# Two weight blocks kept in PSUM: other blocks, other slots, and three small moves in the loop's dependency chain

## The chip, the cores and the metric

One core of a Trainium2 chip. The metric is the device time of one execution in microseconds; lower is better. In this kernel TensorE does the matrix products, VectorE, ScalarE and GpSimd the copies and the softmax, and SyncE issues the transfers (DMA) from HBM, the memory off the core; SBUF is the on-chip memory that holds the weights, PSUM the smaller one that the products write to. Where I quote a ratio, it is the mean time of one kernel's fast runs over that of the other kernel's fast runs of the same rounds, so it is not quite the ratio of the medians beside it. Sessions ran on different chips (the kernel before had medians from 2851.5 to 2869.2 us in them), so kernels are compared by their ratios to the kernel before, or within one session.

Times inside a step are counted from the write of `hT`, the first thing that the next step's products need. Where I say "mean of the steps", I took the trace's records of 58 or 59 steps and laid them over each other at that write; first and last packets of a block were found by counting the 4096-byte packets, 128 to a block, in the order of their starts, and are medians over the steps. Issue times are means.

## The reference, cut to what matters

Two independent parts are joined along the last axis. Part B is a long convolution that the change does not touch. Part A is attention with a memory that is handed from one segment of 32 rows to the next, so its 64 steps run one after the other:

```python
mem = mem0
for s in range(n_seg):                                  # 64 steps
    h = concatenate([mem, x[s]], axis=1)                # 8 + 32 rows
    q, k, v = (einsum('btd,dhe->bhte', h, W) for W in (Wq, Wk, Wv))
    p = softmax(where(mask, q k^T * scale, -1e9))
    o = einsum('bhqk,bhke->bhqe', p, v)
    o = einsum('bhte,hed->btd', o, Wo)
    mem = o[:, :8, :]                                   # the next step waits for this
    outs.append(o[:, 8:, :])
```

Each step needs all four weights, 64 blocks of [128, 2048] bf16 (512 KB). They do not all fit on chip.

## The kernel before: what the change touches

46 of the 64 blocks stay in SBUF for the whole loop. 16 are streamed from HBM in every step, in a fixed order, through four buffers ("slots") in turn. The last two are *kept*: they lie in PSUM, and VectorE copies each of them in every step to one of the four slots, after that slot's streamed block was used and before its next load.

```python
STREAM = {("k", 0): (0, 6), ("q", 0): (3,), ("k", 1): (0, 4), ("q", 1): (0, 4), ("v", 0): (0, 4), ("v", 1): (0, 4)}
STREAM_O = (0, 4, 8, 11, 14)
KEPT = {("k", 0, 4): ("o", 14), ("q", 0, 5): ("k", 0, 6)}    # kept block: whose slot it is copied to
SLOTS = 4

def unit(key):                                 # the weights of one block, just before their products
    if key in W_res: return W_res[key]
    if key in kept:  return ahead_of.pop(key)
    between.pop(key, lambda: None)()           # other DMAs that go into the queue ahead of this load
    place[key] = loads[0] % SLOTS; loads[0] += 1
    t_ = wst.tile([128, 2048], BF16, name="wst", tag="w%d" % place[key])
    nc.sync.dma_start(out=t_[:], in_=WD[key][:])
    return t_

def fetch(key):                                # copy a kept block, as int32 words, into a slot
    t_ = wst.tile([128, 2048], BF16, name="wst", tag="w%d" % place.get(KEPT[key], SLOTS - 1))
    for n in range(2):
        words(t_[:, 1024 * n:1024 * n + 1024], kept[key][n][:])
    ahead_of[key] = t_
```

All loads go through one queue, SyncE's, in program order. A load waits there until its slot is free, and every later load waits behind it. With 16 loads and four slots, slot 0 takes in each step k0's first block, k1's fifth, v0's fifth and o's fifth; slot 1, among others, k0's seventh and q1's first; slot 2 q0's fourth and q1's fifth; slot 3 k1's first, v0's first and the last streamed o block (the names of the loads in a step are, in order: k0_0, k0_6, q0_3, k1_0, k1_4, q1_0, q1_4, v0_0, v0_4, v1_0, v1_4, o0, o4, o8, o11, o14). I use these names below, and the same kind of name for kept blocks.

The step itself (cut; `...` marks cuts):

```python
between["k", 1, 0] = lambda: stores(s - 1, ob)          # the last step's two stores, ahead of k1_0
a = quads("k", 0, range(KC))
...
fetch(("q", 0, 5))
k0 = evac(a, "A")
...
a = quads("k", 1, H0); ...; quads("k", 1, H1, a)        # H0 = 0..3, H1 = 4..7
...
tr(p1, 0, k1, KT1[:, :, :, 0:SL])                       # VectorE copies the transposes
S0 = softmax_b(st0, ex0)
...
L0 = left_blocks(S0)
quads("v", 0, H1, a); V0 = evac(a, "A")
sc1 = scores(1, QT1, KT1); st1, ex1 = softmax_a(sc1)
...
nc.vector.tensor_copy(out=hT[:, :, XM:SL]..., in_=pt_o[...])   # the hT write
fetch(("k", 0, 4))
```

## Time and profile before

| | before |
|---|---|
| device time, median of 3 | 2859.5 us |
| loop, period of a step (mean of 62) | 27.37 us |
| weights streamed in a step | 16 x 512 KB |
| DMA engines idle in a step (mean of the 16) | 2.66 us |
| of that, excess in the 2nd to 4th us after the hT write | 0.74 us |
| TensorE waits for streamed blocks | 3.7 us a step |

The lines behind it are in the prediction. The rows of idle time are no lines of a view: they are 16 less the number of packets of SyncE's queue under way, summed over time, divided by 16, as a mean of the steps.

### The profile page before, as it was taken

What the parts mean: (1) busy time and instruction counts of PE and PEld (TensorE: products, weight loads), DVE (VectorE), ACT (ScalarE), POOL (GpSimd) and SP (SyncE); (2) the same over time, 40 slices, a digit from 0 to 9 for tenths busy, and PEclk for the clock granted to TensorE, in tenths of its full rate; (3) what the DMA queues carried; (4) which work ended last, traced back from release to release, by engine and by line L of the source; (5) the groups of instructions that cost most, each with busy time, mean ns of one, the idle gap of its engine ahead of it and who ended that gap; (6) DMA issues with size and microseconds to landing.
All of it is one profiled execution on the core that took longest, in us unless ns stands there. A gap on an engine that the chain in (4) does not pass through costs nothing. (4 is left out here: it accounts for less than half of the span.)

```text
span 2863.4 us, 75870 instructions
## 1 busy us (share of the span) xinstructions
PE 2100.6 (73%) x32791; PEld 1102.1 (38%) x32838; DVE 1511.0 (53%) x2882; ACT 976.7 (34%) x1458; POOL 365.3 (13%) x545
## 2 busy tenths in 40 slices
PE   1478777756797478778777877887787777778747
PEld 0246444542243134344443443443444434344323
DVE  7577677765985145445444444444444444454430
ACT  4767688751121122222222222222222222222220
POOL 2254444542000100000000000000000000000000
PEclk8699888977899799999999999999999999999978
DMA  4556554525345899989989999998999998999991
GB/s 111 149 153 171 168 165 128 148 78 162 99 133 187 318 321 329 320 305 332 320 316 332 329 320 320 327 339 298 330 319 311 331 317 315 320 328 336 322 315 42
DMA packets 377504, 734.83 MB, mean 257 GB/s; under 512 B 115958, under 2 KB 208118, under 8 KB 375120
## 3 DMA queue, kind: packets, MB, share of 16 engines
q1 hardware_dynamic: 352866, 679.52, 70.4%
q0 software_dynamic: 8528, 28.41, 2.8%
q10 hardware_dynamic: 15774, 22.03, 2.4%
q8 instruction: 257, 4.21, 0.6%
q14 instruction: 79, 0.65, 0.1%
HBM read 675.04 MB, written 67.37 MB: 259 GB/s over the span
## 5 line engine op out<-in xcount | busy, mean ns | idle before, releaser
L310 PE MATMUL acc<-wst,hT 128*32 128x512 bf16 x3328 | 371.0, 402 | 235.1 <-DMA wst<-WD_k 132.8
L310 PEld LDWEIGHTS <-hT 128*32 128x32 bf16 x12288 | 318.7, 98 | 560.7 <-issue 288.5
L316 ACT CAST ev<-acc 128x512 bf16<-128x512 f32 x384 | 225.1, 586 | 511.5 <-PE acc L310 509.0
L409 PEld LDWEIGHTS <-oT 128*32 128x32 bf16 x8192 | 204.2, 96 | 169.8 <-issue 119.8
L310 PE MATMUL acc<-W_q,hT 128*32 128x512 bf16 x3072 | 242.6, 390 | 0.0
L310 PE MATMUL acc<-W_k,hT 128*32 128x512 bf16 x2816 | 237.4, 404 | 0.0
L409 PE MATMUL pp<-W_o,oT 128*32 128x256 bf16 x5632 | 223.0, 273 | 0.0
L261 DVE TENSOR_SCALAR wst<-keep 128x512 int32<-128x512 int32 x256 | 165.0, 686 | 106.8 <-PE acc L310 82.9
L310 PE MATMUL acc<-W_v,hT 128*32 128x512 bf16 x3072 | 213.6, 382 | 0.0
L348 DVE TENSOR_REDUCE mx<-sc 128x8 f32<-128x320 f32 x128 | 62.3, 487 | 242.2 <-PE sc L341 242.1
L409 PE MATMUL pp<-wst,oT 128*32 128x256 bf16 x2560 | 128.0, 276 | 77.7 <-DMA wst<-WD_o 64.7
L322 DVE COPY KT<-tr 128x512 bf16<-128x512 bf16 x128 | 54.4, 425 | 211.7 <-PE tr L321 211.7
L329 POOL COPY KT<-pk 128x128 bf16<-128x128 bf16 x128 | 37.6, 294 | 898.0 <-PE sc L341 554.2
L322 ACT COPY QT<-tr 128x512 bf16<-128x512 bf16 x128 | 74.9, 585 | 213.2 <-PE tr L321 204.7
L483 DVE CAST ob<-pp 128x128 bf16<-128x128 f32 x64 | 18.7, 292 | 243.4 <-issue 239.7
L1075 PE MATMUL yp<-Bt,mi 128*128 128x512 bf16 x379 | 112.2, 399 | 35.3 <-DVE Bt L1029 17.9
L993 PE MATMUL hps<-KT,MF 128*128 128x512 bf16 x374 | 100.4, 413 | 51.0 <-DVE x L1004 27.0
L396 ACT CAST oT<-pv 128x512 bf16<-128x512 f32 x128 | 75.2, 588 | 182.3 <-PE pv L382 177.2
L288 POOL COPY hT<-xt 128x192 bf16<-128x192 bf16 x64 | 22.2, 347 | 813.4 <-DMA xt<-XTd 623.0
L350 ACT ACTIVATE sc<-sc 128x320 f32<-128x320 f32 x128 | 54.0, 422 | 204.5 <-DVE sc L349 181.5
L129 PE MATMUL pro<-xTl,wsl 128*128 128x512 bf16 x492 | 113.6, 380 | 8.8 <-DVE ua L782 4.6
L877 DVE SCALAR_TENSOR_TENSOR nr<-kM,ptt 128x656 f32<-128x656 f32 x128 | 106.1, 829 | 22.8 <-ACT kM L876 19.4
(263 smaller groups left out, 3729.8 us busy)
## 6 DMA issues: line engine op xcount, KB each, us to landing
wst<-WD_o SPq DMA_DIRECT2D x320, 512.0 KB
wst<-WD_k SPq DMA_DIRECT2D x256, 512.0 KB
wst<-WD_v SPq DMA_DIRECT2D x256, 512.0 KB
wst<-WD_q SPq DMA_DIRECT2D x192, 512.0 KB
Ud<-ux POOLq DMA_DIRECT2D x16, 1024.0 KB, 5.8
uq<-Ud SPq DMA_DIRECT2D x32, 512.0 KB
pk<-PKd SPq DMA_DIRECT2D x64, 192.0 KB
wsl<-in_A_Wk_dram SPq DMA_DIRECT2D x16, 512.0 KB
```

What stands on the lines that cost most here:

```text
L129: nc.tensor.matmul(a[:], lhsT=w[:, kc, 128 * j:128 * j + 128], rhs=xTl[:, kc, :, :].rearrange("p s k -> p (s k)"), start=(kc == 0), stop=( ...
L261: nc.vector.tensor_scalar(out=out.bitcast(I32), in0=in_.bitcast(I32), scalar1=0, scalar2=None, op0=ALU.bitwise_or)
L310: nc.tensor.matmul(a[32 * g:32 * g + 32, :], lhsT=hT[:, kc, :], rhs=w[:, 512 * g:512 * g + 512], start=(kc == 0), stop=(kc == KC - 1), til ...
L316: nc.scalar.copy(out=q[:], in_=a[:])
L322: eng(out=dst, in_=p[:, i, :, :, :])
L348: nc.vector.tensor_reduce(out=mx[:], in_=sc, axis=AX.X, op=ALU.max)
L350: nc.scalar.activation(out=sc, in_=sc, func=ACT.Exp, scale=scale)
L396: nc.scalar.copy(out=o[:], in_=p[:].rearrange("p a (g q) -> p a g q", g=4))
L409: nc.tensor.matmul(po[32 * qt:32 * qt + 32, :], lhsT=oT[:, h % 4, (h % 16) // 4, :], rhs=w[:, 1024 * hh + 256 * qt:1024 * hh + 256 * qt + ...
L877: v.scalar_tensor_tensor(out=nrs[e // 4][:, e % 4].rearrange("p f t j -> p f (t j)"), in0=kM[:], scalar=MAGIC, in1=ptv, op0=ALU.subtract, ...
L993: pe.matmul(ps[:], lhsT=MF[:, 4 * rr + mc, cs, 128 * kc:128 * kc + 128], rhs=rhs, start=(i == 0 and mc == 0), stop=(i == 1 and mc == 3))
L1075: pe.matmul(yp[:], lhsT=m_[:, cs, kc, :], rhs=Bt[:, kc, half, j, c_, :], start=(n == 0), stop=(n == 15))
```

## The change

Its intent: the copy at the step's end holds the slot of o14 until k0's fifth block has been used, so k1_0 cannot be asked for before that. The change keeps other blocks, whose copies go to slots that free later in the step, and shortens VectorE's dependency chain by three moves. The core of the diff:

```diff
-KEPT = {("k", 0, 4): ("o", 14), ("q", 0, 5): ("k", 0, 6)}
+KEPT = {("q", 0, 0): ("k", 0, 0), ("k", 1, 6): ("k", 1, 0)}
...
-            p = (ps_pv, ps_sc)[t].tile([128, 4, 128], F32, name="pv", tag=("pv", "sc")[t])
+            p = (ps_o, ps_sc)[t].tile([128, 4, 128], F32, name="pv", tag=("pp", "sc")[t])
...
-        fetch(("q", 0, 5))
+        fetch(("q", 0, 0))
...
         a = quads("k", 1, H0)
+        fetch(("k", 1, 6))
...
-        tr(p1, 0, k1, KT1[:, :, :, 0:SL])
+        tr(p1, 0, k1, KT1[:, :, :, 0:SL], nc.scalar.copy)
...
-        L0 = left_blocks(S0)
         quads("v", 0, H1, a)
         V0 = evac(a, "A")
         sc1 = scores(1, QT1, KT1)
         st1, ex1 = softmax_a(sc1)
+        L0 = left_blocks(S0)
...
+        o0 = evac_o(pv0, "B")          # ahead of the second half of v1 and of pv_l
+        quads("v", 1, H1, a)
+        V1 = evac(a, "E")
...
-            fetch(("k", 0, 4))
```

More of the change, by code (lines that the diff above doesn't have):

```diff
@@ L270, in fetch @@
     def fetch(key):
-        t_ = wst.tile([128, 2048], BF16, name="wst", tag="w%d" % place.get(KEPT[key], SLOTS - 1))
+        t_ = wst.tile([128, 2048], BF16, name="wst", tag="w%d" % place[KEPT[key]])
         for n in range(2):
@@ L463, in part_a @@
         pv_l(pl_, 0, V0, L0)
-        o0 = evac_o(pv0, "A")
-        quads("v", 1, H1, a)
-        V1 = evac(a, "E")
         S1 = softmax_b(st1, ex1)
@@ L474, in part_a @@
         pv1 = pv_x(1, V1, pk[:, 0:512].rearrange("p (a b) -> p a b", a=4), [lb1[:].rearrange("p a k -> p (a k)")])
-        o1 = evac_o(pv1, "B")
+        o1 = evac_o(pv1, "A")
         oproj(pp[:, 1, :], (7,), o0)
@@ L489, in part_a @@
             nc.vector.tensor_copy(out=hT[:, :, XM:SL].rearrange("p (q j) r -> p j q r", j=2), in_=pt_o[:, :, :, XM:SL])
-            fetch(("k", 0, 4))
         nc.scalar.copy(out=ob[:, 1, :], in_=pp[:, 0, :])
```

## The prediction

> **What bounds the kernel now.** I read the page's forty slices first, then the DMA queue's own timeline, a step boundary cut into windows of a microsecond, the waits of TensorE, and last the VectorE timeline inside a step. The page:
>
> ```profile
> span 2863.4 us, 75870 instructions
> PE 2100.6 (73%) x32791; PEld 1102.1 (38%) x32838; DVE 1511.0 (53%) x2882; ACT 976.7 (34%) x1458; POOL 365.3 (13%) x545
> ...
> DMA  4556554525345899989989999998999998999991
> GB/s 111 149 153 171 168 165 128 148 78 162 99 133 187 318 321 329 320 305 332 320 316 332 329 320 320 327 339 298 330 319 311 331 317 315 320 328 336 322 315 42
> ```
>
> The reader is to see two programs in one: to about slice 13 the part that the change leaves alone, then the loop with the DMA engines at 90% and over and some 320 GB/s. The loop writes hT once a step; the first and last such records lie at 1036.6 and 2733.4 us with 62 periods between: 27.37 us a step, from 25.7 to 30.0. Each step streams 16 blocks of 512 KB through four slots, 8.39 MB. So the loop (64 steps, 1752 us of 2863) lives by its weight stream, and the change can give what the stream loses, and little else.
>
> Where it loses is at the step's boundary (SyncE's queue, then windows from the hT write at 2022.25; columns: busy PE, PEld, DVE, ACT, POOL, clock, DMA share, GB/s):
>
> ```profile
> 2019.60 0.32 SPq L239 DMA_DIRECT2D wst<-WD_q  x1
> 2022.04 0.32 SPq L297 DMA_DIRECT2D OLd<-ob  x1
> 2022.45 0.55 SPq L299 DMA_DIRECT2D out_dram<-ob  x1
> 2023.94 0.79 SPq L239 DMA_DIRECT2D wst<-WD_k  x2
> ```
>
> ```profile
> 2016.00:2022.00 6.00, 4.54 (x108) 2.76 (x100) 1.98 (x5) 1.11 (x3) 0.35 (x1) 1.00 0.98 362
> ...
> 2024.25:2025.25 1.00, 1.00 (x20) 0.49 (x20) 0.64 (x2) 0.42 (x1) 0.00 (x0) 1.00 0.84 163
> 2025.25:2026.25 1.00, 1.00 (x20) 0.52 (x19) 0.65 (x2) 0.16 (x1) 0.00 (x0) 1.00 0.76 209
> ```
>
> No weight block is issued from 2019.60 to 2023.94, and two microseconds later the rate has fallen from 362 to 163 and 209 GB/s. Laying 59 steps over each other by the hT write, the mean idle time of an engine is 0.04 to 0.12 us in each microsecond, except 0.23, 0.56 and 0.13 in the second, third and fourth: an excess of 0.74 us. Packets there are also slower to start, another 0.2. TensorE pays for it at the first block after the hole, then drifts along with the stream:
>
> ```profile
> PE acc L310 <- DMA wst<-WD_k: 85.5, 88, 2.5
> PE pp L409 <- DMA wst<-WD_o: 59.8, 104, 1.9
> PE acc L310 <- DMA wst<-WD_q: 38.9, 74, 2.4
> PE acc L310 <- DMA wst<-WD_v: 28.0, 37, 2.0
> PE tro L488 <- DVE ob L483: 26.5, 58, 0.8
> PE pv L378 <- DVE pk L364: 25.0, 39, 0.8
> PE sc L334 <- DVE pt L359: 10.8, 34, 0.3
> PE pv L378 <- DVE L L367: 6.3, 25, 0.3
> ```
>
> (1100 to 2700 us, some 58 steps): 212 us of DMA waits, 3.7 a step, against 42 us, 0.7 a step, for the products' operands from VectorE (the last three).
>
> **What the Trainium skill says.** "DMA: Bandwidth & Descriptors", Specifications, gives about 358 GB/s of HBM for a core and 0.6 us to the first byte of a hardware-issued DMA. The trace agrees: 362 GB/s in the full stretch, and on the mean of the steps 0.58 us from the end of the issue of the first block after the hole (2.18 after the hT write) to its first packet (2.76). Anatomy of one DMA says that DMA engines do not wait on semaphores, the issuing sequencer does, and that the write receipt delays completion. Here, from a block's last packet to TensorE's use of it, where it waited for it, the mean is 1.3 us (k1's first: 5.04 to 6.32). So a block whose slot is held also holds every later issue of the queue. "PSUM — Partial Sum Buffer", Specifications, has no DMA access to PSUM: a block kept there must go through an engine. The trace shows it as VectorE's copies, two of 686 ns each.
>
> **The change, part by part.**
>
> 1. *Kept blocks.* Two of 64 blocks of weights sit in PSUM and are copied to a slot each step. Before, k0's fifth goes to the slot of the last o block, after the hT copy, and k1's first stream block cannot be issued until TensorE has used it; that is the hole. After, that slot is free at the last o product, 1.4 us before the hT write, and k1's first follows the two stores directly. The stores' issue ends at 0.75 (mean), so it issues by 1.1, first packet 1.7 at the earliest; the block before it (first packet 0.35, plus 1.52 us a block, plus some of the stores' 0.4) is through at 2.0. That hole closes: 0.74 us.
>  But the copied blocks now hold other slots. q0's first sits in the slot of k0's first, which the second block of k1 needs. TensorE reaches it at about 2.6 (k0's streamed block lands at 0.7, usable at 2.0 to 2.15, two keys later), is done with it by 3.1, and the stream block goes out: 3.1 + 0.36 (matmul end to issue end, 1.82 to 2.18 before) + 0.58 = 4.05. The stream wants it at 2.0 + 1.5 = 3.5. A hole of 0.5 in the earliest engine, and since a block's first and last packets lie 0.4 apart in skew beyond its 1.52, about 0.35 on the mean.
>  The seventh of k1 sits in the slot of k1's first, which v0's first needs. TensorE uses k1's second stream block 3.07 after its first packet (4.80 to 7.87 before), the kept one two keys (0.42) on, and 0.45 for its matmuls: 3.95; plus 0.94 gives 4.9, where three blocks of the stream take 4.55. A hole of 0.3 in the earliest engine, 0.15 on the mean. Before there was 1.6 us of slack at this place (issue 7.13, first packet 9.36).
>  Sum: 0.74 - 0.35 - 0.15 = 0.24 us a step.
>  The copies themselves cost nothing: q0's first can be copied once k0's first is used (0.6) and is ready at 2.0, needed at 2.6; k1's seventh follows the KT copy and takes 5.9 to 7.3, needed at about 7.7. The same 2.6 us of VectorE as before.
> 2. *Second keys' copy on ScalarE.* 425 ns leave VectorE, 585 come to ScalarE, which is 34% busy. VectorE runs in order and its first sum of exponentials stands behind that copy: it starts at 13.04 while the exponentials are done at 11.25 (means). So the chain sum, reciprocal, product, two transposes, two left operands, pb comes up to 1.7 us earlier.
> 3. *Left blocks later.* Two of 281 ns move behind the second score reduction and subtraction, into the 0.55 us in which VectorE waits for the second exponential. The second softmax starts up to 0.5 us earlier.
> 4. *First products in another bank, evacuated before the left product.* The second softmax's transposes no longer share a bank with the first products. In the trace that wait is hardly there (0.13 us before L358), so about nothing by itself.
>  Parts 2 to 4 together can remove TensorE's 0.43 (pk), 0.18 (pt), 0.11 (L) and 0.17 (oT) us of means a step, 0.9 us at most. Most of it ends in the next DMA wait: o blocks wait 0.53 us for the last and 0.2 for two others. It counts in full only where TensorE sets the pace: 19 of the 60 steps that I looked at have a granted clock under 0.96; they take 28.1 us against 27.05 of the others, with TensorE busy 22.7 against 21.3 and the DMA engines no busier (24.9 against 25.1). A third of 0.8 is 0.27 us a step.
>
> Sum: 0.24 + 0.27 = 0.5 us a step; 64 steps make 33 us; 2859.5 - 33 = 2827. I say 2830, as some of the second term may vanish into DMA waits even there.
>
> **The rivals.**
> - *The hole closes and no new one opens.* For it: VectorE is ready in time, and the skew among the 16 queues may hide both waits. Gain 0.74 + 0.2 a step, 60 us, with part 2 to 4 more: about 2790. Against it: the issue order is fixed, and k1's second block waits in that order for q0's first.
> - *The holes only move.* If the two new waits cost their full 0.5 and 0.3, nothing is left of 0.74, and parts 2 to 4 vanish in DMA waits: 2850 to 2860. Against it: the new holes are shorter than the one removed, and the earlier softmax releases o slots sooner.
> - *Worse.* The copy of k1's seventh waits for k1's first to be used; a late first block delays the copy by 1.4 us, then TensorE and v0's load wait for it: up to 0.5 us a step, 2880 or above. Against it: k1's second stream block lands later than that copy ends in most steps.
>
> **Range and chances.** The spread is that of the two holes: 0.8 us less hole to none, with 0 to 0.5 from VectorE's parts. I put 8 in 10 on 2798 to 2856. Faster by over 2% means below 2802.3, 0.9 us a step, which needs the first rival nearly whole: 0.12. Slower by over 2% needs the third: 0.03. Within 2%: 0.85.
>
> **What would show it.** In the changed profile the weight issue after the two stores should follow within half a microsecond; the idle of the DMA engines in the second to fourth microsecond should shrink to some 0.35 with a smaller hole about v0's first block. Waits of TensorE for WD_k should fall from 85 us to about 55, those of pv for pk to near zero, and the DVE chain should stand a microsecond earlier, with WD_o waits larger. The period should be near 26.9 us. I am wrong if the period falls below 26.5 (the new holes do not exist), if it stays at 27.3 (they cost all), or if TensorE waits on VectorE's wst copies.

## The result, and the profile after

The changed kernel takes 2930.7 us (median of 4, 2918.1 to 2940.0) against 2858.4 of before; the ratio is 1.0259, with a 95% interval of 1.0208 to 1.0311. That is slower by more than 2%, to which the prediction had given 0.03, and 75 us above the upper end of its range.

The same lines of the page, after:

```profile
span 2933.8 us, 75932 instructions
PE 2139.6 (73%) x32791; PEld 1118.0 (38%) x32838; DVE 1498.6 (51%) x2818; ACT 1016.3 (35%) x1522; POOL 363.3 (12%) x545
...
DMA  4555653534347888899989888999898889988891
GB/s 113 157 154 154 181 151 110 158 99 136 99 138 247 297 306 308 316 317 316 309 307 317 309 307 308 321 319 319 304 322 310 310 304 319 305 308 310 291 314 49
```

The copies moved as the diff says (64 of 425 ns from VectorE to ScalarE, where one takes 591; the page's DVE time falls by less, as it counts overlapping records once). What differs is the stream: eights among the nines, some 310 instead of 320 GB/s. The period of a step is 28.34 us, 0.97 more than before; 64 times that is 62 us of the 72. In this profile the first hT write of the loop also came 8.5 us later (1045.1 us); in the other profiles it comes anywhere from 1032 to 1044 us.

The queue's own timeline at one step boundary (hT write at 1976.13, a step of 28.2 us at full clock). The columns are start, duration, instruction; an issue that waits in the queue shows as a long duration:

```profile
1973.38 0.32 SPq L239 DMA_DIRECT2D wst<-WD_q  x1
1975.91 0.32 SPq L295 DMA_DIRECT2D OLd<-ob  x1
1976.33 0.55 SPq L297 DMA_DIRECT2D out_dram<-ob  x1
1976.97 2.96 SPq L239 DMA_DIRECT2D wst<-WD_k  x2
1979.99 0.90 SPq L239 DMA_DIRECT2D wst<-WD_q  x2
1984.54 3.15 SPq L239 DMA_DIRECT2D wst<-WD_v  x4
```

k1_0 now follows the stores at once, as intended. The next one, k1_4, is in the same row, and its issue ends only at 1979.93. Then two blocks for q1, and nothing for 3.7 us until v0_0. The same step in windows of a microsecond (busy PE, PEld, DVE, ACT, POOL, clock, DMA share, GB/s):

```profile
1979.13:1980.13 1.00, 0.96 (x23) 0.41 (x16) 0.00 (x0) 0.59 (x1) 0.00 (x0) 1.00 0.79 299
1980.13:1981.13 1.00, 1.00 (x20) 0.40 (x19) 0.00 (x0) 0.00 (x0) 0.00 (x0) 1.00 0.63 152
...
1984.13:1985.13 1.00, 1.00 (x45) 0.43 (x38) 0.00 (x0) 0.31 (x1) 0.00 (x0) 1.00 0.88 360
1985.13:1986.13 1.00, 0.61 (x35) 0.32 (x20) 0.65 (x2) 0.27 (x1) 0.30 (x1) 1.00 0.61 147
1986.13:1987.13 1.00, 0.77 (x16) 0.29 (x12) 0.45 (x2) 0.42 (x1) 0.00 (x0) 1.00 0.99 328
```

There are two holes now, each some half a microsecond to a microsecond after a late issue: rate 152 at 1980, and 147 at 1985. TensorE's waits from 1100 to 2700 us (total, times, longest):

```profile
PE acc L308 <- DMA wst<-WD_k: 88.4, 89, 2.9
PE pp L407 <- DMA wst<-WD_o: 84.5, 120, 2.1
PE acc L308 <- DMA wst<-WD_v: 74.9, 75, 3.1
PE acc L308 <- DMA wst<-WD_q: 27.8, 49, 1.7
...
PE pv L380 <- DVE lb L365: 5.8, 27, 0.2
```

Against the same rows of before, WD_v rose from 28.0 to 74.9 us: that is v0_0, the load of the second hole. WD_k stayed near 86. The waits for pk, pt and L from VectorE, 42 us before, are gone, and only 6 for lb are there instead. WD_o rose by 25. So the three moves did what they were to do to these waits, and the waits for the o blocks grew.

As mean of the steps, the idle time of the DMA engines in each microsecond after the hT write (worked out from the records):

```
us after the hT write   1     2     3     4     5     6     7     8     9     10    11    sum of the step
before                .07   .23   .56   .13   .04   .04   .12   .07   .04   .04   .06   2.66
after                 .11   .36   .10   .12   .53   .14   .06   .05   .20   .41   .25   3.59
```

The idle time rose by 0.93 us a step, and the period by 0.97. The packets of 4096 bytes took only 0.12 us a step longer than before (3.32 against 3.20 us above 159 ns each).

A second difference is TensorE's granted clock. In the loop (1100 to 2700 us, with the same columns as above; first before, then after) it is 0.97 and 0.94:

```profile
1100.00:2700.00 1600.00, 1270.26 (x24859) 644.50 (x24858) 757.79 (x1819) 416.80 (x819) 54.48 (x175) 0.97 0.92 323
1100.00:2700.00 1600.00, 1252.20 (x23987) 632.10 (x23983) 720.47 (x1694) 437.53 (x849) 53.31 (x170) 0.94 0.89 312
```

Of the 62 periods, 19 had a mean granted clock under 0.96 before (28.10 us, the others 27.04) and 40 after (28.63 and 27.81). So by an estimate from these figures some 0.3 us of the 0.97 (21 of 62 steps, times 0.8 to 1.1 us) go with the larger number of such steps; why there are more is not shown. The holes do not need it: in the steps at 0.96 or more the idle time rose by 0.80 us and the period by 0.77. The rest of this document asks what made these holes.

### The profile page after: what moved, and what is told of

It reads as the page before. It is cut to its first block, busy times and chain, and to the rows that moved or that the text cites. A ratio compares the mean times of both kernels' runs of the same rounds, so it can differ in the third digit from the quotient of the medians.

```text
span 2933.8 us, 75932 instructions
## 1 busy us (share of the span) xinstructions
PE 2139.6 (73%) x32791; PEld 1118.0 (38%) x32838; DVE 1498.6 (51%) x2818; ACT 1016.3 (35%) x1522; POOL 363.3 (12%) x545
## 5 line engine op out<-in xcount | busy, mean ns | idle before, releaser
L308 PEld LDWEIGHTS <-hT 128*32 128x32 bf16 x12288 | 337.3, 101 | 622.3 <-issue 333.9
L308 PE MATMUL acc<-wst,hT 128*32 128x512 bf16 x3328 | 359.7, 415 | 289.8 <-DMA wst<-WD_k 139.7
L308 PE MATMUL acc<-W_k,hT 128*32 128x512 bf16 x2816 | 247.2, 436 | 0.0
L308 PE MATMUL acc<-W_q,hT 128*32 128x512 bf16 x3072 | 226.9, 397 | 0.0
L308 PE MATMUL acc<-W_v,hT 128*32 128x512 bf16 x3072 | 221.0, 393 | 0.0
L320 DVE COPY KT<-tr 128x512 bf16<-128x512 bf16 x64 | 27.2, 425 | 217.5 <-PE tr L319 217.5
L874 ACT ACTIVATE kM<-ptt,magic 128x656 f32<-128x656 f32 x128 | 103.4, 808 | 21.3 <-PE ptt L855 21.2
```

The costliest lines, as they stand in the source:

```text
L308: nc.tensor.matmul(a[32 * g:32 * g + 32, :], lhsT=hT[:, kc, :], rhs=w[:, 512 * g:512 * g + 512], start=(kc == 0), stop=(kc == KC - 1), til ...
L320: eng(out=dst, in_=p[:, i, :, :, :])
L874: sc.activation(out=kM[:], in_=ptv, func=ACT.Identity, bias=magic[:])
```

## The experiments

The theories: **S**, the slots. A kept block holds its slot from the last use of the slot's streamed block to its own use; where this is longer than the slack of the slot's next load, the stream gets a hole. **R**, the rest: the moves to ScalarE and to the other bank lengthen the step. **C**, the copies: VectorE's copying itself, or its traffic, costs.

### Which part of the change costs

**Only the rest.** The changed kernel with the old kept blocks put back:

```diff
-KEPT = {("q", 0, 0): ("k", 0, 0), ("k", 1, 6): ("k", 1, 0)}
+KEPT = {("k", 0, 4): ("o", 14), ("q", 0, 5): ("k", 0, 6)}
 # and the three fetch() calls where the kernel before has them
```

> The changed kernel with the kept blocks of before put back (k0's fifth and q0's sixth): only the ScalarE copy, the later left blocks and the other bank are new. Theory S (the slots that the copied blocks hold open two holes in the weight stream, and these are the whole loss): 2830 to 2860 us, within 1% of before or a little faster; the DMA engines' idle time near the hT write as in before (excess 0.7 us a step), no hole before v0's first block. Rival R (the moves to ScalarE and the other bank make the step longer): 2890 us or more, over 1.5% slower than before.

Measured: 2845.1 us, ratio 0.9978 (0.9922 to 1.0035): same as before. The idle profile is that of before (0.34, 0.71, 0.21 in the second to fourth microsecond, nothing later). TensorE's waits:

```profile
PE pp L409 <- DMA wst<-WD_o: 89.9, 142, 2.5
PE acc L310 <- DMA wst<-WD_k: 69.4, 81, 2.2
...
PE acc L310 <- DMA wst<-WD_v: 28.2, 42, 1.8
```

WD_v is at its old 28, so the hole at v0 does not come from these parts. The 42 us of waits on VectorE are gone here too, and WD_o rose from 59.8 to 89.9: most of what VectorE no longer costs comes back as waits for the o blocks.

**Only the kept blocks.** The KEPT line and the fetch() calls of the change on the kernel before.

> The kernel before with only the kept blocks and their slots changed (q0's first, k1's seventh). Theory S: at least as slow as the whole change, 2925 to 2970 us, with holes before k1's second and v0's first streamed block. Rival R: 2880 us or less.

Measured: 2903.5 us, ratio 1.0170 (1.0126 to 1.0214), with both holes (idle 3.60 us a step). That is below what I had expected for S and above what R allowed. The whole change had shown 1.0259 in its session, so I could not tell if its other parts cost another 0.9% under the new slots. I therefore ran both once more on one chip.

> The whole change once more, beside its kept blocks alone on the same chip, to see if its other parts cost anything under the new slots (1.026 against 1.017 in two sessions). If the difference is of the sessions: the two agree within 0.5%. If the other parts cost under the new slots: the whole change 0.7% or more slower than its kept blocks alone.

> The kept blocks alone, for that comparison: 1.017 to 1.026 of before.

Measured: 1.0266 (1.0220 to 1.0313) for the whole change, 1.0285 (1.0243 to 1.0328) for its kept blocks alone. No cost of the other parts shows beside it; the difference was one of sessions. R falls.

### Which hold costs

**Without the first hold, without the second, without both.** In the changed kernel a kept block is read from its resident neighbour: no copy, no hold. The result is wrong. (The comparison with the reference still passed in these runs; its tolerance does not see one block of 64 exchanged, so it proves nothing about them.)

```diff
+        if key == ("q", 0, 0):
+            return W_res["q", 0, 1]
 # second run: key == ("k", 1, 6) from W_res["k", 1, 7]; third run: both; the fetch() of it taken out
```

> The changed kernel, in which q0's first block is read from its resident neighbour instead (a wrong result on purpose): no copy of it and no slot held; k1's seventh stays as it is. Theory S with both holes costing: about 0.5 us a step less, 2885 to 2905 us, and k1's second streamed block issued within 0.6 us of k1's first. If only the hole before v0's first costs: 2920 or more. Rival R: no change, 2920 to 2940.

> The changed kernel, in which k1's seventh block is read from its resident neighbour instead (a wrong result on purpose): no copy and no hold of the slot of k1's first. Theory S: the hole of 0.7 us before v0's first block goes, 2880 to 2900 us. If only the hole before k1's second costs: 2920 or more. Rival R: no change.

Measured: without q0_0's hold 2854.2 us, 1.0024 (0.9956 to 1.0092); without k1_6's hold 2854.6 us, 0.9999 (0.9945 to 1.0054). Against the whole change in the other sessions (1.0259, 1.0266) each brings back 2.3 to 2.7%, about the whole loss; against the kept blocks alone in their own session (1.0170), 1.5 and 1.7%. Both are more than I had expected of either. The wait for v0_0 tells the two apart; first without q0_0's hold, then without k1_6's:

```profile
PE acc L310 <- DMA wst<-WD_v: 89.7, 89, 2.6
```

```profile
PE acc L310 <- DMA wst<-WD_v: 29.4, 39, 1.5
```

The second hole is k1_6's: with its hold alone the wait stays, without it the wait is as before. In the idle profile each run has lost its own hole and kept the other (0.9 us in the ninth and tenth microsecond together; 0.8 us in the fourth and fifth). The profiled execution without q0_0's hold was the slowest of its four (2886.3 us, the others 2844.8 to 2856.4), so its period is not used.

> The changed kernel with both copied blocks read from resident neighbours (a wrong result on purpose): no copies, no slot held. Theory S: both holes and most of the boundary's idle gone, DMA idle 2.2 us a step or less, period 26.2 to 26.7 us, 2780 to 2820 us. If the two single removals do not add up because another bound is reached: 2840 to 2855.

Measured: 2817.8 us, 0.9819 (0.9760 to 0.9878), period 26.27 us in the profiled run, idle 1.90 us a step, no hole but 0.33 in the second microsecond. The profiled execution was the fastest of the four (2799.4 us, the others 2816 to 2823). The two removals add up within the noise, and what is left is a kernel 1.8% faster than before: that much comes of holding no slot, with the stores where they were. Nor is it the clock: in the steps with a granted clock of 0.96 or more the period is 27.81 us with both holds, 27.06 and 26.71 with one of them removed, 26.02 with none.

### The hold or the copy

**A fifth tile for the copies.** Both copies are still made, at the same places, but into a tile of their own. SBUF has no room for it, so v1's eighth block is read from its neighbour (wrong).

```diff
-        t_ = wst.tile([128, 2048], BF16, name="wst", tag="w%d" % place[KEPT[key]])
+        t_ = wst.tile([128, 2048], BF16, name="wst", tag="own")
```

> The changed kernel, both copies still made on VectorE at the same places of the program, but into a fifth tile of their own, so that they hold no slot of the stream; the room comes from reading v1's eighth block from its neighbour (a wrong result on purpose). Theory S (the hold costs, the copy not): within 0.7% of the run with both copies removed, 2780 to 2830 us. Rival C (the copy itself costs, by VectorE's time or by its traffic): 2860 us or more, most of the loss of the change still there.

Measured: 2810.3 us, 0.9803 (0.9753 to 0.9854), as without any copy. The copies are there, and each takes what it took before:

```profile
L263 DVE TENSOR_SCALAR wst<-keep 128x512 int32<-128x512 int32 x224 | 143.2, 681 | 0.0
```

So the copy costs nothing that shows, and the hold costs. C falls.

### Why the second hole is so long

**k1's third block instead of its seventh.** The seventh is used after k1_4 has landed; the third needs only k1_0, whose slot it takes.

```diff
-... ("k", 1, 6): ("k", 1, 0)}
+... ("k", 1, 2): ("k", 1, 0)}
-        a = quads("k", 1, H0)
-        fetch(("k", 1, 6))
+        a = quads("k", 1, range(0, 1))
+        fetch(("k", 1, 2))
+        quads("k", 1, range(1, 4), a)
```

> The whole change, but with k1's third block in place of its seventh as the one copied into the slot of k1's first. If the hole before v0's first block comes of waiting inside the hold for k1's second stream block to land: v0's first issued at about 8.0 us instead of 9.2, the hole of 0.7 us goes, 2860 to 2895 us, near the run without that hold (1.000 of before). If any copy into that slot costs the same: 2915 to 2940. TensorE may now wait up to 1 us for the copy; that should not show, since it would wait for the landing anyway.

Measured: 2885.1 us, 1.0091 (1.0031 to 1.0150). v0_0 is issued at 8.14 us instead of 9.19, and idle in the ninth to eleventh microsecond falls from 0.86 to 0.34 in sum. Against the change in its other sessions that is a gain of 1.7% for one index, but not the whole hold's 2.6%: TensorE now waits for the copy, and v0 is not fully cured:

```profile
PE acc L308 <- DMA wst<-WD_v: 60.7, 89, 2.6
PE acc L308 <- DVE wst L261: 44.8, 114, 0.6
```

I had written that this wait would not show, since TensorE would wait for k1_4 anyway; 45 us over some 58 steps show that the order matters. So waiting for a landing inside the hold made most of the second hole.

### What the hole that the change removed was worth

**The kernel before without k0_4's hold** (wrong, as above):

> The kernel before, with k0's fifth block read from its neighbour (a wrong result on purpose): no copy at the boundary, no hold of the last o block's slot. If the hole at the boundary is worth its 0.74 us of idle: period 26.8 us, about 2815 us, 1.5% faster. If closing it only lets the stream meet q0's sixth, held before q1's first, earlier: 0 to 0.7% faster, with idle in the fifth to seventh microsecond.

Measured: 2842.2 us, 0.9931 (0.9878 to 0.9985), period 26.88 us. A hole of 0.74 us, closed outright, is worth 0.7%, 20 us, and not 64 x 0.74 = 47. The idle profile tells why: 0.28 (0.04 before) appears in the sixth microsecond, at q1_0, which waits for q0_5 in the slot of k0_6. The stream, now earlier, meets the next hold earlier. In the profiled runs, the idle of a step fell by 0.35 us in all (2.66 to 2.31). The ratio lies at the edge of what I had expected (0 to 0.7%), and the profiled run (2830.9) was the fastest of its four, so I take the ratio and not the period.

### Versions meant to beat both

**The last o block kept, stores later.** k0_4's copy is replaced by one of o's sixteenth block into the slot of o11, while VectorE idles, and the stores go behind k1_0.

```diff
-KEPT = {("k", 0, 4): ("o", 14), ("q", 0, 5): ("k", 0, 6)}
+KEPT = {("o", 15): ("o", 11), ("q", 0, 5): ("k", 0, 6)}
-            between["k", 1, 0] = lambda: stores(s - 1, ob)
+            between["k", 1, 4] = lambda: stores(s - 1, ob)
```

> The kernel before, in which the block copied at the step's boundary is the last o block instead of k0's fifth, copied into the slot of the fourth streamed o block while VectorE idles, and the two stores are issued behind k1's first block. Theory S: the boundary hole of 0.74 us goes and none opens, since that slot's next load had over 2 us of slack: period 26.6 to 26.9 us, 2810 to 2835 us, k1's first block issued before the hT write. Against it: the last o block waits for its copy or the hole moves to q0's streamed block: 2855 or more.

> The same kept blocks and late stores with the change's other parts (ScalarE copy, later left blocks, other bank). Theory S: equal to the one without them or up to 0.5% faster, 2800 to 2835 us. If those parts cost anything once the stream is even, as the whole change against its kept blocks alone hints (1.026 against 1.017 of before): 0.5% slower or more.

Measured: 1.0172 (1.0105 to 1.0239) and, with the change's other parts, 1.0074 (1.0014 to 1.0134). Both miss. The first shows its reason in TensorE's waits:

```profile
PE acc L308 <- DMA wst<-WD_q: 118.2, 118, 3.2
```

q0_3 is the next load of the held slot; its issue moved from -2.42 to -0.86 us. I had reckoned 2 us of slack, but TensorE then waits 1.08 us for it (mean of the steps; 0.03 before), reaches q0_5 later, and q1_0 goes out at 5.82 instead of 5.02 us, with 0.5 us of idle in each of the sixth and seventh microseconds. A late block lengthens the next hold. Here the other parts seem worth 1%, but the intervals overlap.

**Blocks that are used soon after their copy.** k0_5 in k0_0's slot and q0_4 in k0_6's, with the change's other parts; then with the stores behind k1_0.

```diff
+KEPT = {("k", 0, 5): ("k", 0, 0), ("q", 0, 4): ("k", 0, 6)}
-        a = quads("k", 0, range(KC))
+        a = quads("k", 0, range(0, 4))
+        fetch(("k", 0, 5))
+        quads("k", 0, range(4, KC), a)
```

> The change's other parts, with two other blocks kept, chosen so that each copied block is used soon after its copy can end: k0's sixth in the slot of k0's first (copied while TensorE waits for k0's streamed seventh) and q0's fifth in the slot of k0's seventh. Theory S (a hold costs only what it takes beyond the slack of that slot's next load): the hole before k1's second block nearly goes (its issue at about 2.9 instead of 3.64 us after the hT write), q1's first is issued at about 4.8, wanted at 5.0; DMA idle 2.1 to 2.4 us a step, 2805 to 2835 us, 1 to 2% faster than before. If holds cost whatever their length: 2850 or more.

> The same with the two stores issued behind k1's first block, so that this block is asked for before the hT write. Theory S: the 0.3 us of idle left in the second microsecond goes, but as in the last-o-block run an earlier stream meets the next hold sooner (q0's fifth before q1's first): between 0.5% faster and 0.5% slower than the run with the stores ahead.

Measured: 1.0150 (1.0110 to 1.0190) and 1.0013 (0.9972 to 1.0053). The first is well off my expectation: q1_0 was issued at 5.21 us and not 4.8, since the two copies stand one behind the other on VectorE until 4.33 us and TensorE waits for them. That wait is only 10 us in the loop, though; TensorE's waits for WD_q rose from 39 to 84 us, so the copies are not shown to be the whole reason. But its idle was only 2.85 us a step, 0.19 more than before, and its 4096-byte packets together 0.35 us a step slower than before (3.56 us above 159 ns each, against 3.20). So a part of this loss is not idle time. In the steps with a granted clock of 0.96 or more its period is that of before (27.09 against 27.04 us); the loss lies in the steps below, 34 of 62 against 19.

**Short holds.** q0_2 instead of q0_4, and each copy half by VectorE and half by ScalarE:

```diff
-        for n in range(2):
-            words(t_[:, 1024 * n:1024 * n + 1024], kept[key][n][:])
+        words(t_[:, 0:1024], kept[key][0][:])
+        nc.scalar.copy(out=t_[:, 1024:2048].bitcast(F32), in_=kept[key][1][:])
```

> The other parts of the change, late stores, and two kept blocks with short holds: k0's sixth (slot of k0's first) and q0's third (slot of k0's seventh), each copied half by VectorE, half by ScalarE. The rule: copies end 0.7 us after the slot is free, k1's second block issued by 2.4, q1's first by 4.2, both inside the slack of about 1.6 us: no hole, idle 2.0 us a step, period 26.3 to 26.7, 2795 to 2825 us, 1.2 to 2.2% faster than before and close to the runs that hold no slot. If not: 2845 or more.

> The same with the stores ahead of k1's first block as in both kernels: the idle of 0.3 us in the second microsecond stays, 2805 to 2840 us.

Measured: with the stores behind k1_0 2827.7 us, 0.9900 (0.9851 to 0.9949), correct, the fastest true kernel, 1.0% faster than before: clear of noise. q1_0 goes out at 4.41 us, k1_4 at 2.66, idle is 2.27 us a step. Around a step of it (hT write at 1938.85):

```profile
1937.46 0.32 SPq L239 DMA_DIRECT2D wst<-WD_k  x1
1938.63 0.32 SPq L295 DMA_DIRECT2D OLd<-ob  x1
1939.01 0.55 SPq L297 DMA_DIRECT2D out_dram<-ob  x1
1940.63 0.33 SPq L239 DMA_DIRECT2D wst<-WD_k  x1
1942.40 1.75 SPq L239 DMA_DIRECT2D wst<-WD_q  x2
```

k1_0 is asked for 1.4 us ahead of the hT write and k1_4 1.8 us behind it; no issue around the hT write waits 3 us any more. It fell just short of what I had expected (1.2 to 2.2%). With the stores ahead of k1_0 the same kernel is at 1.0026 (0.9970 to 1.0082), 1.3% slower than with the stores behind, where I had expected half a per cent. The pair before shows 1.4%. In both pairs the version with the stores ahead has more idle in the second microsecond (0.39 against 0.02 here) and slower packets over the step (3.49 against 3.12 us above 159 ns each here). Why the packets are slower I did not find out. More steps fall under a granted clock of 0.96, too (43 of 62 against 32), and the steps above it differ by only 0.18 us (26.45 against 26.27).

## Why the prediction was wrong

- *What bounds the kernel*: right. The stream's idle time rose by 0.93 us a step and the period by 0.97. The 362 GB/s that the prediction set beside the skill's 358 is no ceiling, though: single microseconds reach 406 GB/s after the change (1976.13 to 1977.13).
- *Where the holes would be*: right in place and cause. The prediction named k1_4 behind q0_0 and v0_0 behind k1_6, and said that v0_0's slot is held over k1_4's landing. The removals of each hold, the fifth tile and the run with k1's third block show all of it.
- *"That hole closes: 0.74 us"*: this failed by 0.3. k1_0's first packet came at 2.10 us and not 1.7, and 0.30 us of excess stayed in the second microsecond. The stores stand ahead of it in the queue; in the four runs with k1_0 ahead of them that idle is gone.
- *"A hole of 0.5 in the earliest engine ... about 0.35 on the mean"*: mis-sized. k1_4 was issued at 3.64 us, as reckoned within 0.2, but its first packet came at 4.53 and not at 4.05. The stream wanted it 1.52 us after k1_0's first packet at 2.10, so the hole in the earliest engine was 0.9. The excess idle in the fourth to sixth microsecond is 0.61 us on the mean (0.12 + 0.53 + 0.14, less 0.06 each).
- *"A hole of 0.3 in the earliest engine, 0.15 on the mean"*: the worst term. From k1_4's first packet to v0_0's it took 5.3 us (4.53 to 9.87) and not 4.9, where the stream wanted 4.55: a hole of 0.8. The excess in the ninth to eleventh microsecond is 0.68 us (0.20 + 0.41 + 0.25, less 0.06 each).
- The step that failed is the same in both: the way from the hold's end back to a running stream was reckoned too short. *"0.58"* from the end of an issue to its first packet was a median less a mean; taken within each step, the means are 0.74 us at that place before, and 0.91 (k1_4) and 0.89 (v0_0) after. *"3.07 after its first packet"*, from a block in the full stream to TensorE's use of it, has a mean of 2.98 us before and of 3.34 after (3.12 in the repeat of the change), when the stream has just run dry. The cut from the earliest engine to the mean was about right for the first hole (0.9 to 0.61) and too large for the second (0.8 to 0.68, where 0.3 was cut to 0.15). So the sum is not 0.74 - 0.35 - 0.15 = +0.24 but (0.74 - 0.30) - 0.61 - 0.68 = -0.85 us a step, and 64 of these are 54 us of the 72 lost.
- *The copies themselves cost nothing*: right, by the run with the fifth tile.
- *"A third of 0.8 is 0.27 us a step"* for the other parts: not shown. They took the waits on VectorE away, as predicted, and WD_o rose by 30 us in the run of the rest alone, as predicted too; but the time moved by 0.2%, with an interval that holds zero, and the low-clock steps gained no more than the others (28.10 to 27.45 us against 27.04 to 26.42, in one profiled execution each, on different chips), where the prediction had put the whole gain there.
- *The rivals*: the third, with k1_6's hold delaying v0_0, was the nearest. It named the right wait and, at "2880 or above", the right side; its trigger, a late copy, was the wrong one, since the copy ends at 7.4 us and TensorE comes to k1_6 at 8.4. It was held to be rare because k1_4 lands later than the copy. That very lateness was the cost.
- The first rival, no new hole and "about 2790", was too high a hope as well: with no hold at all the kernel is at 0.9819 of before, which is 2808 of 2859.5 us (the interval just reaches 2791), and removing the old hole alone is worth 0.7%, since the stream then meets the next hold sooner.

What stays open: why packets are slower in some of these kernels than in others (2.7 to 3.6 us a step above 159 ns each; the same kept blocks alone had 3.11 in one session and 3.40 in the other), and why more steps have a lowered clock after the change. The first carries 0.12 us of the 0.97, the second some 0.3 by the estimate above, part of it as idle time.

## What to carry to other kernels

In a ring of buffers that one ordered queue refills, ask of every extra tenant of a slot when it is *used*, not how long its copy takes, and compare the time to that use with the slack of the slot's next load; if another transfer has to land before that use, the stream is tied to its own latency and runs dry. A hole's length does not say what its removal gives: the old one, 47 us in 64 steps, gave 20, as the stream then met the next hold sooner; the two new ones, 39 and 44 us, gave 42 to 76. And spans measured in a full stream were too short here for one that restarts. When a change moves the limiting stream, test it first with the holds taken away by wrong data: two such runs told here what holding no slot is worth (1.8 and 2.0%), though not what moving the stores adds.

## What the Trainium skill lacked or had wrong

- "DMA: Bandwidth & Descriptors", Specifications, gives 0.6 us to the first byte of a hardware-issued DMA. Here, taken within each step, the first packet after a hole came 0.66 us after the end of the issue before (k1_0), and 0.77 us after the change (k1_4 and v0_0), by medians; the means are 0.74, 0.91 and 0.89. The page has one figure and does not say how far single loads lie above it.
- The same page, Anatomy of one DMA, fits about 2.0 us of fixed cost for the software path, most of it the write receipt. Here, on the hardware path, a mean of 1.15 us passed from a block's last packet to its use (k1_0 before; TensorE waited for it in 53 of 60 steps). The page gives no such figure for this path, nor for a ring of slots, where it lengthens every hold that spans a landing.
- No page that I found says what two small stores ahead of a load in the same queue cost. Moving them behind one load was worth 1.4% (1.0150 to 1.0013) and 1.3% (1.0026 to 0.9900), with quicker packets of the loads (3.12 against 3.49 us a step above 159 ns each, in the second pair).
- "PSUM — Partial Sum Buffer", Specifications, gives DMA no access to PSUM, which no run here tries. As a place to keep weights PSUM cost no measurable time for the copy itself (0.9803 with copies into a tile of their own, 0.9819 without copies), which no page says.
